# Attention gated by a spatial-shift MLP: small activations in front of more table loads, and a new order of the same instructions

## The chip, the cores and the metric

One of the eight cores of a Trainium2 chip. The metric is the device time of one execution in microseconds (us), median of several runs. Inputs and output are f32.

## What is computed

The reference, cut to what matters (S = 2048 rows, D = 512, H = 32 heads of 16, F = 1376):

```python
xn  = layernorm(x)
# A: linear attention without a mask
q, k, v = split(xn @ wqkv)                     # 32 heads of 16
phi = lambda t: where(t > 0, t + 1, exp(t)) + 1e-6
kv  = phi(k).T @ v;  z = sum(phi(k))           # per head
s   = (phi(q) @ kv / (phi(q) @ z + 1e-6)) @ wo
# B: spatial-shift MLP
h   = gelu(layernorm(xn) @ w1)                 # four quarters of columns, shifted by +1, -1, +2, -2 rows
x1  = xn + shifted(h) @ w2
g   = silu(x1 + gelu(layernorm(x1) @ w3) @ w4)
out = x + s * g
```

## The kernel before

The 2048 rows are 16 tiles of 128, in four quarters of four tiles. Every matmul of full accuracy is made of products of a rounded high part and a low part of each operand (`products`, L343), and many of the 2x2 block products are done with seven products in place of eight (`seven`), whose sums and differences VectorE (DVE) and ScalarE (ACT) make.

The first half of the time goes to layer norms, k, q, the Gram matrices of phi(k) with the rows, and the token mixing (w1, w2). From about 220 us on each quarter b runs through its groups of columns of the 1376: `up_pair` (L1256, w3, GELU), `turn_q` and `forms_q` (phi(q) over its denominator, transposed by way of a round trip to DRAM), `attend_pair` (L1426, the attention rows `so`), `downs` (w4), and last `gate` (L1444), which takes SiLU of the sum (`th<-e`), multiplies by `so` and adds x.

Names that the steps below speak of: `th5_0` and `th10_0` are the SiLU results of row tiles 5 and 10 (L1452, an activation recorded with table 2); `e` is the sum that they read; `p`, `u`, `gf` are copies of PSUM banks (`pb`, `pe`, `pa`) that the seven products of `up_pair` sum in; `so` is the same for the attention; `qr` and `pq` are phi(q)'s two parts from `qv`, a fetch; `yb122h`, `yb122l` are the high and low part of a sum of the layer-normed rows; `w_0h`, `w_0l`, `w_1h`, `w_1l` are sums of blocks of w4, which go to DRAM (`w4t`) and come back; `f_2a`, `f_2sh`, `f_2sl`, `f_3a` are GELU results and their sums; `q9t` is the transposed phi(q) of tile 9, in four fetches from `q9d`, and `q8f`, `q8s0h` are sums of it for the matmuls `pes`, `pbs`; `kt` at the start is k with its mean taken off, which frees the PSUM bank of k for q; `mv` are means. The page leaves the numbers in the names out.

Nothing is emitted as it is written down. `Plan.add` (L99) records 5566 instructions with what each reads and writes. `Plan.emit` (L234) then emits them in the order of a long table, `ORDER`, and gives each tile the slot that a second table, `HOMES`, names: 98 row buffers of 128x512 (tag p), some smaller ones, and eight PSUM banks. Five engines take their own instructions from that order: PE (TensorE), DVE, ACT, POOL, and SP, whose queue issues the DMAs (L217 loads, L221 stores, L225 fetches of what was stored; L229 adds by DMA on POOL). The waits between engines follow from the reads, the writes and the earlier users of a slot.

Activations belong to three tables: Exp, GELU and SiLU (0, 1, 2, L167). Where the table changes, the compiler puts a table load (ACT_TABLE_LOAD) in front of the activation, and the load takes over waits of that activation. `op.warm` (L178) is a one-column activation with the same function, from a constant `tiny` into a column `scr` that nothing reads: it is emitted in front of the real user, so that the load stands in front of it. Before the change `emit` does this (L251) only where the user waits for at least two engines other than ScalarE. `engs` there is the set of engines of the instructions that the user depends on, and of those that used its slot before.

Of the kernel before, what the change touches and what calls it, by code (L numbers as in the profile page):

```python
# [88 lines left out]
class Plan:  # L89
# [144 lines left out]
    def emit(self, order, homes):  # L234
# [3 lines left out]
        table = 0  # L238
        for n in order:
            op = self.ops[n]  # L240
            engs = {o.eng for o in op.pre}
            for t in op.tiles:
                if t.ap is None:
                    tag = t.tag
                    if tag in self.counts:
                        tag += str(next(homes))
                        engs |= users.get(tag, set())
                        users[tag] = t.engs
                    t.ap = self.pools[t.tag].tile([t.rows, t.width], t.dtype, tag=tag, name=t.name)
            if op.table is not None:  # L250
                if op.table != table and len(engs - {"ACT"}) > 1:  # L251
                    op.warm()
                table = op.table
            op.emit()
            for t in op.tiles:
                t.engs.add(op.eng)
# [3 lines left out]
def linear_attn_gated_by_mixer(  # L260
# [1364 lines left out]
    for b in range(NQ):  # L1625
# [499 lines left out]
```

## Time and profile before

| | |
|---|---|
| median of 3 runs | 504.7 us (503.86, 504.7, 506.14) |
| the profiled execution | 504.21 us, its span 502.1 us, TensorE clock 1.0 |
| matmuls, and PE busy | 3204 records, 492.3 us |
| weight loads busy | 446.3 us |
| VectorE, ScalarE, GpSimd busy | 455.2, 400.6, 79.0 us |
| DMA | 124.04 MB, mean 247 GB/s |
| table loads on ScalarE | 27, of which 12 in front of a one-column activation |

How to read it: matmuls overlap, so a busy PE is not a PE at its peak. A matmul of 512 columns follows the one before in 0.23 us and one of 256 columns in 0.12 us where nothing holds it up, though the record of one is 0.28 to 0.40 us long; time is lost where starts lie further apart. In rows of the timeline the columns are start (us), duration (us), engine, line, operation, output and inputs with shapes; in brackets the engine's idle time before it and what released it. A line of the waits says which instruction of which engine waited for which, in total, how often, and the longest.

### The profile page before, as it was taken

The page shows a single profiled execution, that of the slowest core. Times are in us where ns is not written, and L with a number is a line of the kernel's source. Part 1 is how long each engine was busy: PE and PEld are TensorE (multiplying, and loading weights), DVE is VectorE, ACT ScalarE, POOL GpSimd, SP SyncE. Part 2 cuts the span into 40 slices and gives each one's busy share as a digit, 9 for nine tenths or more (in the row PEclk, how much of TensorE's full clock was granted, in tenths as well). Part 3 has the DMA queues.
Part 4 walks back from the last instruction along what each step waited for, and adds up shares of the span by engine and source line. Part 5 has one row for each costly group of instructions (what it writes and reads, how often), then busy time and mean ns, then how long its engine had stood idle before and what let it go on. Part 6 is the DMA issues. An engine that isn't in the chain of part 4 may idle for free.

```text
span 502.1 us, 9824 instructions
## 1 busy us (share of the span) xinstructions
PE 492.3 (98%) x3204; PEld 446.3 (89%) x3204; DVE 455.2 (91%) x977; ACT 400.6 (80%) x874; POOL 79.0 (16%) x98
## 2 busy tenths in 40 slices
PE   8999999999999999999999999999999899999996
PEld 7778878888998889999989999999899899899996
DVE  6999989997899999999999998987899988899966
ACT  6999999967898889879777678757599757799553
POOL 1242222121122201430000002200020011200021
PEclk9999999999999999999999999999999999999999
DMA  7969997698999999899898589998689979879655
GB/s 252 343 162 232 245 241 167 171 262 270 302 315 233 279 295 286 197 277 270 289 319 258 176 240 287 323 233 268 229 194 269 297 210 288 273 195 323 187 97 125
DMA packets 95278, 124.04 MB, mean 247 GB/s; under 512 B 9728, under 2 KB 48156, under 8 KB 95228
## 3 DMA queue, kind: packets, MB, share of 16 engines
q1 hardware_dynamic: 85292, 105.33, 66.2%
q0 software_dynamic: 9936, 18.09, 21.5%
q8 instruction: 25, 0.41, 0.3%
q14 instruction: 25, 0.20, 0.1%
HBM read 78.42 MB, written 35.54 MB: 227 GB/s over the span
## 4 chain that ended last, share of the span: by engine, by line
PE 88%; DMA 5%; ACT 3%; DVE 2%; issue 1%; SPq 0%; ACTq 0%; DVEq 0%
PE a L151 12%; PE pb L151 9%; PE g L151 9%; PE pbk L151 7%; PE acc L151 6%; PE pe L151 5%; PE pbm L151 5%; PE h L151 4%; PE pbs L151 4%; PE uc L151 4%; PE pek L151 3%; PE pa L151 2%; PE pes L151 2%; PE pem L151 2%; PE pbg L151 2%; PE q L151 2%
## 5 line engine op out<-in xcount | busy, mean ns | idle before, releaser
L229 POOL DMA_DIRECT2D th<-in_x x14 | 12.3, 977 | 130.4 <-DVE xo L198 55.7
L229 POOL DMA_DIRECT2D e<-x1d x12 | 10.5, 990 | 100.9 <-DMA q11d<-q11z 39.2
L173 ACT ACT_TABLE_LOAD x15 | 19.2, 1283 | 7.3 <-DVE e L198 3.8
L229 POOL DMA_DIRECT2D zacc<-kr x16 | 17.1, 1069 | 49.8 <-DVE kr L208 17.9
L229 POOL DMA_DIRECT2D o<-x x16 | 14.3, 922 | 56.3 <-ACT o L173 22.5
L173 ACT ACTIVATE gf<-gf 128x256 f32<-128x256 f32 (+1 forms) x50 | 22.3, 457 | 0.5
L491 POOL TENSOR_TENSOR rs<-w,nhalf 128x4 f32<-128x4 f32 (+2 forms) x10 | 12.0, 1205 | 29.9 <-DVE w L203 29.9
L178 ACT ACT_TABLE_LOAD x12 | 15.4, 1283 | 0.2
L198 DVE TENSOR_TENSOR th<-th,so 128x512 f32<-128x512 f32 (+1 forms) x17 | 11.0, 658 | 2.9 <-ACT th L173 2.7
L173 ACT ACTIVATE y<-o,nm,rs 128x512 f32<-128x512 f32 x16 | 12.7, 806 | 0.6 <-DVE nm L208 0.6
L173 ACT ACTIVATE x<-x,nm,rs 128x512 f32<-128x512 f32 x16 | 12.8, 804 | 0.0
L208 DVE SCALAR_TENSOR_TENSOR kr<-kt,kr 128x512 f32<-128x512 f32 x16 | 10.9, 687 | 1.5 <-ACT kr L173 1.1
L173 ACT ACTIVATE p<-pe 128x256 f32<-128x256 f32 x20 | 7.6, 380 | 5.5 <-PE pe L151 5.4
L173 ACT ACTIVATE p<-pb 128x256 f32<-128x256 f32 x20 | 7.6, 380 | 4.9 <-PE pb L151 4.9
L208 DVE SCALAR_TENSOR_TENSOR qz<-pq,zb 128x512 f32<-128x512 f32 x16 | 10.9, 682 | 0.1
L198 DVE TENSOR_TENSOR gf<-pa,p 128x256 f32<-128x256 f32 x20 | 8.3, 417 | 3.0 <-PE pa L151 1.3
L1378 DVE TENSOR_REDUCE den<-qz 128x32 f32<-128x512 f32 x16 | 10.8, 676 | 0.1
L208 DVE SCALAR_TENSOR_TENSOR pq<-pq,rd 128x512 f32<-128x512 f32 x16 | 10.8, 681 | 0.1
L478 DVE BATCH_NORM_STATS2 st<-o 128x6 f32<-128x512 f32 x16 | 10.8, 681 | 0.0
L198 DVE TENSOR_TENSOR e<-a,e 128x512 f32<-128x512 f32 (+1 forms) x17 | 9.9, 590 | 1.0 <-PE a L151 1.0
L198 DVE TENSOR_TENSOR gf<-pb,p 128x256 f32<-128x256 f32 x20 | 8.4, 420 | 2.2 <-PE pb L151 1.7
L173 ACT ACTIVATE pq<-qv,rk 128x512 f32<-128x512 f32 x12 | 8.5, 712 | 2.2 <-DMA w4t<-w_1l 1.4
(1967 smaller groups left out, 2368.8 us busy)
## 6 DMA issues: line engine op xcount, KB each, us to landing
w_s<-in_w SPq DMA_DIRECT2D x36, 256.0 KB
w_t<-w4t SPq DMA_DIRECT2D x32, 256.0 KB
w_b<-w4d SPq DMA_DIRECT2D x30, 256.0 KB
x<-in_x SPq DMA_DIRECT2D x16, 256.0 KB
zacc<-kr POOLq DMA_DIRECT2D x16, 256.0 KB, 6.7
o<-x POOLq DMA_DIRECT2D x16, 256.0 KB, 5.1
w1t<-w1d SPq DMA_DIRECT2D x16, 256.0 KB
x1d<-o SPq DMA_DIRECT2D x16, 256.0 KB
```

What stands on the lines that cost most here:

```text
L151: lambda: nc.tensor.matmul(out.get(), lhs.get(), rhs.get(), start=start, stop=stop, skip_group_check=more))
L173: nc.scalar.activation(out.get(), src.get(), func, scale=get(scale), **kw)
L178: op.warm = lambda: nc.scalar.activation(self.scr[1].get(), self.scr[0].get(), func)
L198: self.vec(eng, out, [a, b], lambda: self.e(eng).tensor_tensor(out.get(), a.get(), b.get(), op=op), True)
L208: lambda: self.nc.vector.scalar_tensor_tensor(out.get(), a.get(), get(s), b.get(), op0=op0, op1=op1),
L229: lambda: self.nc.gpsimd.dma_start(out.get(), get(src), accum_op=ALU.add))
L478: pl.add("DVE", .62, .69, [xv], [st], lambda: nc.vector.bn_stats(st.get(), xv.get()))
L491: lambda: g.tensor_tensor(out.get(), src.get(), nh.get(), op=ALU.pow))
L1378: pl.add("DVE", .6, .68, [t], [den], lambda: nc.vector.tensor_reduce(den.get(), t.get().rearrange("p (h d) -> p h d", d=DH), axis=AX.X, op ...
```

## The change

The condition in `emit` no longer leaves ScalarE out of the set: a small activation now also goes in front of a table change whose user waits for one other engine and for ScalarE itself. `ORDER` and `HOMES` are new tables for the same 5566 instructions: 1738 of the 5566 places hold the same number, and the mean distance that one moved is 2.7 places (the furthest 180); 344 of 1668 entries of `HOMES` are equal. The core of the diff:

```diff
             if op.table is not None:
-                if op.table != table and len(engs - {"ACT"}) > 1:
+                if op.table != table and len(engs) > 1:
                     op.warm()
                 table = op.table
             op.emit()
...
     ORDER = (
         36, 4, 20, 1, 0, 27, 2, 12, 8, 21, 3, 9, 13, 5, 10, 7, 14, 22, 15, 30, 16, 24, 17, 18, 19, 37, 23, 39,
         40, 33, 41, 90, 28, 168, 93, 38, 91, 29, 94, 42, 303, 92, 171, 95, 43, 102, 44, 48, 105, 120, 103, 31,
-        169, 45, 32, 104, 106, 121, 25, 56, 88, 170, 89, 60, 46, 122, 34, 123, 26, 47, 124, 35, 96, 172, 173,
...
```

The number of instructions on PE, VectorE, GpSimd and SP stays. ScalarE keeps its 27 table loads; 19 of them (12 before) stand in front of a small activation. The seven new ones are in front of the users kt8 and kt9 (phi(k) of tiles 8 and 9), f1_0a11, f2_2a11 and f3_0a11 (the first GELU of groups of quarters 1, 2 and 3; f1_0a11 is exchanged with gf1_0, whose load it was), th5_0 and th10_0.

ScalarE at th5_0, near 360 us, before:

```order
L173 ACTIVATE yt42h_5259<-yt4f2_5227 128x512
L173 ACT_TABLE_LOAD
L173 ACTIVATE th5_0_5301<-e11_4573 128x512
L173 ACTIVATE qr8_5314<-qv8_5069,rk_101 128x4x4x32
L173 ACTIVATE p12_0_5316<-pb2_0_5263 128x256
L173 ACTIVATE th6_0_5318<-e12_4720 128x512
```

and now:

```order
L173 ACTIVATE yt42h_5263<-yt4f2_5232 128x512
L178 ACT_TABLE_LOAD
L178 ACTIVATE scr_90<-tiny_86 128x1
L173 ACTIVATE th5_0_5303<-e11_4558 128x512
L173 ACTIVATE qr8_5317<-qv8_5074,rk_101 128x4x4x32
L173 ACTIVATE p12_0_5319<-pb2_0_5260 128x256
L173 ACTIVATE th6_0_5321<-e12_4721 128x512
```

The load moved from th5_0 to the small activation (scr from tiny) ahead of it; what follows keeps its order. At th10_0, near 430 us, it is the same: the load now stands in front of scr, ahead of th10_0, and p13, so11, th9 and u23 keep their places.

PE near 390 us, where the sum a2_10_1 is begun with yb122h (the bank is new to it), before:

```order
L151 MATMUL a3_2_5397<-w4_2_0h_5511,f2_2sh_5737 128x256
L151 MATMUL a3_2_5397<-w4_2_0l_5560,f2_2sh_5737 128x256
L151 MATMUL a2_10_1_5781<-yb122h_5772,w3_lh_3075 96x256
L151 MATMUL pb2_3_5664<-yt32h_5244,w3_3_s1h_3660 128x256
L151 MATMUL pb2_3_5664<-yt32l_5271,w3_3_s1h_3660 128x256
L151 MATMUL pb2_3_5664<-yt32h_5244,w3_3_s1l_3705 128x256
L151 MATMUL a1_2_5437<-w4_2_2_b22_5644,f2_2sh_5737 128x256
L151 MATMUL a2_2_5411<-w4_2_0h_5511,f2_2sl_5739 128x256
```

and now:

```order
L151 MATMUL a3_2_5400<-w4_2_0l_5565,f2_2sh_5742 128x256
L151 MATMUL a3_2_5400<-w4_2_0h_5515,f2_2sl_5744 128x256
L151 MATMUL pb2_3_5667<-yt32h_5246,w3_3_s1h_3662 128x256
L151 MATMUL pb2_3_5667<-yt32l_5280,w3_3_s1h_3662 128x256
L151 MATMUL pb2_3_5667<-yt32h_5246,w3_3_s1l_3720 128x256
L151 MATMUL a1_2_5442<-w4_2_2_b22_5648,f2_2sh_5742 128x256
L151 MATMUL a2_2_5414<-w4_2_0h_5515,f2_2sl_5744 128x256
L151 MATMUL a2_10_1_5809<-yb122h_5778,w3_lh_3076 96x256
L151 MATMUL a2_10_1_5809<-yb122l_5780,w3_lh_3076 96x256
L151 MATMUL a2_10_1_5809<-yb122h_5778,w3_ll_3082 96x256
```

The first matmul of a2_10_1 moved behind six others: w4_2_0h with f2_2sl (two of them, for a3_2 and a2_2), the three of yt32 with w3_3_s1, and w4_2_2_b22 with f2_2sh. On ScalarE at the same place qr10 now goes ahead of pq10, and f2_3a11 ahead of f2_3a22.

VectorE near 16 to 19 us, where kt0 and kt2 take k out of its banks, before:

```order
L198 TENSOR_TENSOR wqt_259<-wq_s0_150,wq_s1_181 128x512
L203 TENSOR_SCALAR w0_280<-mv1_93 128x1
L208 SCALAR_TENSOR_TENSOR kt0_282<-wneg_268,mv1_93,k0_193 128x512
L198 TENSOR_TENSOR wq_1l_293<-wq_s1_181,wq_1h_291 128x512
L203 TENSOR_SCALAR mv1_93<-sx2_289 128x1
L198 TENSOR_TENSOR wqt_259<-wqt_259,wq_s2_195 128x512
L208 SCALAR_TENSOR_TENSOR kt2_317<-wneg_268,mv1_93,k2_146 128x512
```

and now:

```order
L198 TENSOR_TENSOR wqt_245<-wq_s0_150,wq_s1_181 128x512
L203 TENSOR_SCALAR mv1_93<-sx0_257 128x1
L208 SCALAR_TENSOR_TENSOR kt0_284<-wneg_266,mv1_93,k0_194 128x512
L203 TENSOR_SCALAR mv1_93<-sx2_281 128x1
L198 TENSOR_TENSOR wqt_245<-wqt_245,wq_s2_196 128x512
L203 TENSOR_SCALAR w0_296<-mv1_93 128x1
L208 SCALAR_TENSOR_TENSOR kt2_304<-wneg_266,mv1_93,k2_146 128x512
L198 TENSOR_TENSOR wq_1l_306<-wq_s1_181,wq_1h_290 128x512
```

w0 and the low part wq_1l moved behind kt0, wq_1l also behind kt2, and the mean mv1 of tile 0 stands directly ahead of kt0.

Elsewhere: on ScalarE u21_0, near 299 us, stands one place earlier, ahead of th3. On SP, near 401 us, one more fetch (w4_2_10l) stands between the store q9d and the four fetches q9t; the fetch w4_1_0_b21, near 275 us, moved behind the store w4d of w4_8l.

748 rows, old and new, of tables (HOMES, ORDER) are left out of this document.

## The prediction

> **What bounds the kernel now.** I read the page first: the busy shares and the chain of work that ended last.
>
> ```profile
> PE 492.3 (98%) x3204; PEld 446.3 (89%) x3204; DVE 455.2 (91%) x977; ACT 400.6 (80%) x874; POOL 79.0 (16%) x98
> PE 88%; DMA 5%; ACT 3%; DVE 2%; issue 1%; SPq 0%; ACTq 0%; DVEq 0%
> ```
>
> TensorE (PE) sets the time. The change adds and removes no matmul, so all it can give is time in which PE stands still. The waits of PE, grouped by who ended them (total, times, longest), say how much of that the trace names:
>
> ```profile
> PE warm L151 <- POOL ones L379: 1.7, 1, 1.7
> PE a L151 <- ACT pq L173: 1.1, 1, 1.1
> PE pb L151 <- ACT so L173: 0.8, 1, 0.8
> PE pb L151 <- ACT p L173: 0.7, 1, 0.7
> PE q L151 <- DVE mv L203: 0.7, 1, 0.7
> PE uc L151 <- ACT f_3a L173: 0.2, 1, 0.2
> ```
>
> The first is the start, before anything has arrived. The other five are 3.5 us, single events, and I looked for each in the timelines. Last come the table loads of ScalarE (ACT), by the line that caused them (the third column: busy, mean ns; then idle time just before, and its releasers):
>
> ```profile
> L173 ACT ACT_TABLE_LOAD x15 | 19.2, 1283 | 7.3 <-DVE e L198 3.8 <-DVE p1k L198 1.3 <-DVE yt33l L198 1.2
> L178 ACT ACT_TABLE_LOAD x12 | 15.4, 1283 | 0.2
> ```
>
> A load in front of a one-column activation (L178) hardly ever waits; in front of its real user (L173) three of fifteen wait for VectorE (DVE), 3.8, 1.3 and 1.2 us. These three are in reach of the new condition.
>
> **Part 1: the load at 360.74 (th5_0).** ScalarE, VectorE and PE there (start, duration):
>
> ```profile
> 356.35 0.63 ACT L173 ACTIVATE yt42h<-yt4f 128x512 fp32r<-128x512 f32 x1
> 360.74 1.28 ACT L173 ACT_TABLE_LOAD   x1 [3.76 <-DVE e L198]
> 362.03 0.63 ACT L173 ACTIVATE th<-e 128x512 f32<-128x512 f32 x1
> 363.18 0.36 ACT L173 ACTIVATE p<-pb 128x256 f32<-128x256 f32 x1
> ```
> ```profile
> 362.58 0.28 PE L151 MATMUL pe<-yt12h,w_s0l 128*128 128x256 f32 x1
> 363.60 0.39 PE L151 MATMUL pb<-yt22h,w_s0h 128*128 128x256 f32 x1 [0.74 <-ACT p L173]
> ```
>
> The load inherits th's wait for VectorE and stands 3.76 us idle. With a one-column activation ahead, the load runs from about 357.0, and th starts when e is ready, 360.74 instead of 362.03: 1.29 us sooner, and with it qr and p. PE's wait is 0.74; its start-to-start distance is 1.02 where the next matmul of this size follows in 0.12, so the gap costs **0.90** (a wait loses some 0.15 beyond its own length). 1.29 is more than 0.90, so the whole gap goes; the 0.4 left over is slack. A half-way result would need p to be held by its own PE input, and pb is complete long before.
>
> **Part 2: the load at 429.83 (th10_0).**
>
> ```profile
> 428.24 0.39 ACT L173 ACTIVATE p<-pb 128x256 f32<-128x256 f32 x1 [1.37 <-PE pb L151]
> 429.83 1.28 ACT L173 ACT_TABLE_LOAD   x1 [1.21 <-DVE yt33l L198]
> 431.13 0.63 ACT L173 ACTIVATE th<-e 128x512 f32<-128x512 f32 x1
> 431.66 0.37 ACT L173 ACTIVATE so<-pbs 128x256 f32<-128x256 f32 x1
> ```
> ```profile
> 429.07 0.68 DVE L198 TENSOR_TENSOR yt33l<-yt3f,yt33h 128x512 fp32r<-128x512 f32 x1
> ```
> ```profile
> 432.08 0.39 PE L151 MATMUL pb<-yb113h,w_ah 128*128 128x256 f32 x1 [0.75 <-ACT so L173]
> ```
>
> The load can run at 428.63 and end at 429.91; the small activation takes 0.1 more, so th starts at 430.0 instead of 431.13, 1.1 us sooner, and so comes 1.1 us sooner. PE's gap is 0.75 + 0.15 = **0.90** and goes.
>
> The third waiting load (114.74, idle 1.3 behind p1k) has no PE wait near it in the list: 0.
>
> **What the small activations cost.** Seven more, and each takes its place in ScalarE's queue:
>
> ```profile
> 386.72 0.20 ACT L178 ACTIVATE scr<-tiny 128x1 f32<-128x1 f32 x1
> 386.82 0.71 ACT L173 ACTIVATE pq<-qv,rk 128x512 f32<-128x512 f32 x1
> ```
>
> The next instruction starts 0.10 us behind it, so 0.7 us in all on an engine at 80%. Where ScalarE was not idle ahead of the load (f1_0a11 at 299, f2_2a11, f3_0a11 at 434) the user comes 0.1 later. The loads themselves stay 27, the same 1.28 us each. Bounds: 0 to 0.4 on PE; I take 0 here and put it into the allowance below.
>
> By the Trainium skill, "ScalarE: Activation LUTs", section What ACT_TABLE_LOAD costs, a switch of table sets is the load of about 1283 ns and a drain of about 1380 ns, 2.66 us together. The trace has the 1283 but no drain: from the load's start to th's start are 1.29 us (360.74 to 362.03). By the page part 1 would still gain, part 2 not; this is taken up among the rivals.
>
> **Part 3: the new order.** Four exchanges touch gaps of PE. At 390 PE, ScalarE, VectorE and the chain of waits showed:
>
> ```profile
> 384.96 6.07 DMA w4t<-w_1l
> ```
> ```profile
> 391.13 0.72 ACT L173 ACTIVATE pq<-qv,rk 128x512 f32<-128x512 f32 x1 [1.39 <-DMA w4t<-w_1l]
> ```
> ```profile
> 390.08 0.69 DVE L198 TENSOR_TENSOR yb122l<-y_1t,yb122h 128x512 fp32r<-128x512 f32 x1 [0.55 <-ACT w_0h L173]
> ...
> 391.29 0.41 DVE L198 TENSOR_TENSOR gf<-u,pe 128x256 f32<-128x256 f32 x1
> ```
> ```profile
> 390.49 0.28 PE L151 MATMUL a<-w_0l,f_2sh 128*128 128x256 f32 x1
> 391.85 0.33 PE L151 MATMUL a<-yb122h,w_lh 128*96 128x256 f32 x1 [1.08 <-ACT pq L173]
> ...
> 395.25 0.39 PE L151 MATMUL uc<-w_b,f_3a 128*128 128x256 f32 x1 [0.22 <-ACT f_3a L173]
> ```
>
> The wait is put down to pq, but PE's matmul doesn't read pq: it needs yb122 and the bank that gf<-u,pe sets free at 391.70. VectorE is there late: yb122l, ahead of that gf in its queue, takes a slot that the store of w_1h reads, and stores of this stretch land slowly (the row of w_1l's, 6.07 us from its issue, is the nearest). In the new order six matmuls of other sums (w_0h with f_2sl, yt32 with w_s1, w_b22 with f_2sh) stand ahead of a<-yb122h, at 0.12 each **0.7** us of work put into a gap of 1.08 + 0.15. The rest of the gap stays. On ScalarE f2_3a11 now stands ahead of f2_3a22, so the wait at 395.25 (0.22 + 0.15) shrinks, I say by **0.2**. Bounds for both: 0, if a matmul moved ahead waits itself, to 1.6.
>
> At 299 ScalarE's u stood last ahead of the load, and PE waited for its bank:
>
> ```profile
> 298.98 0.36 ACT L173 ACTIVATE u<-pb 128x256 f32<-128x256 f32 x1
> ```
> ```profile
> 299.02 0.28 PE L151 MATMUL pa<-yb211h,w_al 128*128 128x256 f32 x1
> 299.40 0.39 PE L151 MATMUL pb<-yt31h,w_s1h 128*128 128x256 f32 x1
> ```
>
> 0.38 from start to start is 0.26 over the pace. u now stands one place earlier, ahead of a 0.5 us activation: **0.3** back.
>
> At the start kt on VectorE frees the bank for q:
>
> ```profile
> 18.30 0.74 DVE L208 SCALAR_TENSOR_TENSOR kt<-wneg,mv,k 128x512 f32<-128x512 f32 x1
> ```
> ```profile
> 19.09 0.50 PE L151 MATMUL q<-wq_0h,u_0h 128*128 128x512 f32 x1 [0.74 <-DVE mv L203]
> ```
>
> wq_1l (0.7 us) moves from ahead of this kt to behind it, so kt starts about 0.6 sooner; some of PE's work of that stretch moves too, so I count **0.4** of 0.9, bounds 0 and 0.9.
>
> **The sum.** 0.90 + 0.90 + 0.7 + 0.2 + 0.3 + 0.4 = 3.4 us. Against it: the order puts a consumer nearer to its producer at three other places (PE's peg near 124, uc near 470, pb near 474), and the small activations cost something; I charge three waits of the smallest size in the list, 0.2 each: 0.6. That leaves 2.8. The profiled execution took 504.2 (span 502.1): 501.4 for its like. It lay 0.5 under the median of 504.7, so the median is forecast at **501.9**. About 0.5%, 2.5 us, is what a measurement of this kernel can tell from no change: the forecast lies just beyond. Own range 500.4 to 503.3: all bounds of gain with no new waits at one end, half the gain at the other.
>
> **Rivals.**
> - *The exchanges give nothing.* PE's queue is full of reordered work; each moved matmul may meet its own wait. Then only the two loads count: 1.8 less 0.6, **503.5**. For it: DVE is 91% busy. Against: the moved matmuls read operands that lay ready in the trace. 0.11.
> - *The 362 gain is given back at 390.* If the store's landing (6.07 us from issue) clocks that stage, PE arrives 0.9 sooner and waits 0.9 longer: 2.8 less 0.9, **502.8**. Against: the stores are issued behind ScalarE's and VectorE's work, which moves with PE. 0.12.
> - *The change doesn't do what it says.* The activation may inherit the wait itself, or another wait on the load's path (a fetch for qr behind th) ends at the same moment; exchanges nothing: **504.7**. Against: scr and tiny are touched by nothing else late. 0.06.
> - *A drain with each load.* If a load that starts right behind other work held ScalarE for a second 1.28 us, th at 429 would be released at 428.63 + 2.57 = 431.2, no sooner than the 431.13 of now, and part 2 would give nothing: 2.8 less 0.9, **502.8**. The trace speaks against it: scr starts at 386.72, right behind a load, and pq 0.10 later. 0.03. The page of the Trainium skill named above (ScalarE: Activation LUTs) would have it so.
> - *Slower: a fetch comes late.* SP's queue has one more fetch (w_10l) ahead of q9t's four, and q9t feeds VectorE and then PE:
>
> ```profile
> 400.89 0.90 SPq L225 DMA_DIRECT2D q9t<-q9d  x2
> ```
> ```profile
> 405.96 0.42 DVE L198 TENSOR_TENSOR q8f<-q9t 128x256 f32<-128x256 f32 x1
> ```
> ```profile
> 407.94 0.28 PE L151 MATMUL pes<-m_t1h,q8s0h 128*128 128x256 f32 x1
> ```
>
> Two issues take 0.90, so the last goes out 0.45 later, at about 401.8, and must land by 405.96: 4.2 us, then PE stalls. With the 6.07 us of the store it lands at 407.9, 1.9 late, and what VectorE does behind it too; with the gains lost as well, 504.7 + 1.9 = **506.6**, and more if it meets a second one. It decides from a landing of 4.2 us on. For it: DMA engines are busy nearly throughout. Against: before, with 4.6 us, nobody waited, and these fetches are 64 KB. 0.08. By the Trainium skill, "DMA: Bandwidth & Descriptors", a transfer has about 2.0 us of fixed cost and then its bytes at 436 KB per us, some 2.2 us here as an estimate, with which nothing would stall; the 6.07 us of the store speak against it in this stretch.
>
> **How the numbers follow.** The forecast keeps 0.60. The range 500.4 to 505.0 holds it nearly whole, and the first four rivals but for the upper half of the third; it leaves out the slower one and the tails, about 0.15 to 0.2. Faster by over 0.5% means under 502.2: some 0.65 of the forecast's 0.60, and 0.03 from the cases at 502.8, 0.42. Slower means over 507.2: the upper part of the last rival and what I can't see, 0.06. Within 0.5%: 0.52.
>
> **What would show it.** Right: 19 small activations in front of loads; only one load with an idle time of over half a us before it; the waits pb<-p and pb<-so gone from PE's list; the wait at 390 at 0.5 or less; th5_0 starting within 0.1 of the end of e. Wrong, if PE's list has the old waits under new names (pb held by another activation, VectorE's gf later), if the sum of PE's gaps is unchanged, or if a q fetch stands among PE's or VectorE's releasers.

## The result, and the profile after

| | before | after |
|---|---|---|
| median | 504.75 us (503.86 to 506.14, 6 runs) | 501.62 us (501.14 to 502.23, 6 runs) |
| ratio | | 0.9937, 95% interval 0.9922 to 0.9952 |
| profiled execution, its span | 504.21, 502.1 us | 502.23, 500.2 us |

The change makes the kernel 0.63% faster, 3.1 us, where 2.8 us were forecast. The two profiled executions lie only 2.0 us apart; that difference is taken up at the end of the account below.

The same lines of the page after the change:

```profile
PE 492.2 (98%) x3204; PEld 444.4 (89%) x3204; DVE 455.9 (91%) x977; ACT 401.5 (80%) x881; POOL 79.9 (16%) x98
PE 91%; DMA 4%; DVE 2%; ACT 2%; SPq 1%; issue 1%; DVEq 0%
```

The busy time of PE is what it was, and its share of the chain rises from 88 to 91%, while ScalarE's falls. The waits of PE after:

```profile
PE warm L151 <- POOL ones L379: 1.7, 1, 1.7
PE pb L151 <- DVE gf L198: 0.9, 1, 0.9
PE k L151 <- ACT wk_0h L173: 0.3, 1, 0.3
PE q L151 <- DVE kt L208: 0.2, 1, 0.2
```

The waits for p, so, pq and f_3a are gone. A new one has come, pb for VectorE's gf, 0.9. The table loads:

```profile
L178 ACT ACT_TABLE_LOAD x19 | 24.4, 1283 | 0.3
L173 ACT ACT_TABLE_LOAD x8 | 10.3, 1283 | 0.9 <-PEq L2117 0.8
```

Loads that wait for VectorE are no longer there. ScalarE at th5_0 and PE at the place where it waited 0.74:

```profile
358.20 1.28 ACT L178 ACT_TABLE_LOAD   x1
359.49 0.20 ACT L178 ACTIVATE scr<-tiny 128x1 f32<-128x1 f32 x1
361.20 0.64 ACT L173 ACTIVATE th<-e 128x512 f32<-128x512 f32 x1 [1.50 <-DVE e L198]
...
362.52 0.39 ACT L173 ACTIVATE p<-pb 128x256 f32<-128x256 f32 x1
```
```profile
363.15 0.28 PE L151 MATMUL pe<-yt12h,w_s0l 128*128 128x256 f32 x1
363.26 0.28 PE L151 MATMUL pb<-yt22h,w_s0h 128*128 128x256 f32 x1
```

The load is over 1.7 us before e is ready, and PE goes from one matmul to the next in 0.11. At th10_0 it is the same:

```profile
427.50 0.39 ACT L173 ACTIVATE p<-pb 128x256 f32<-128x256 f32 x1 [1.46 <-PE pb L151]
427.90 1.28 ACT L178 ACT_TABLE_LOAD   x1
429.20 0.20 ACT L178 ACTIVATE scr<-tiny 128x1 f32<-128x1 f32 x1
429.31 0.62 ACT L173 ACTIVATE th<-e 128x512 f32<-128x512 f32 x1
429.83 0.36 ACT L173 ACTIVATE so<-pbs 128x256 f32<-128x256 f32 x1
```
```profile
430.35 0.28 PE L151 MATMUL pb<-yb113h,w_ah 128*128 128x256 f32 x1
430.47 0.40 PE L151 MATMUL a<-w_9l,f_9h 128*128 128x512 f32 x1
```

Here th follows scr in 0.11, 1.82 us sooner than before in absolute time and 1.1 sooner behind p (427.50 to 429.31; before 428.24 to 431.13), and PE's matmul has no wait.

At 390 PE now reads:

```profile
390.78 0.28 PE L151 MATMUL a<-w_0h,f_2sl 128*128 128x256 f32 x1
391.21 0.33 PE L151 MATMUL a<-yb122h,w_lh 128*96 128x256 f32 x1
...
392.67 0.27 PE L151 MATMUL a<-yb222h,w_lh 128*96 128x256 f32 x1
393.84 0.38 PE L151 MATMUL pb<-yt42h,w_b 128*128 128x256 f32 x1 [0.89 <-DVE gf L198]
```

The gap in front of a<-yb122h has fallen from 1.24 over the pace to 0.31, as the exchange was to do, and 1.5 us later stands a gap of 1.05 that the profile of before doesn't have. VectorE's gf, and the chain of waits at that place, name the cause of 0.64 of it:

```profile
393.36 0.42 DVE L198 TENSOR_TENSOR gf<-pb,p 128x256 f32<-128x256 f32 x1 [0.64 <-DMA q8d<-q8z]
```
```profile
387.12 6.15 DMA q8d<-q8z
```

gf takes the slot of q8z, which a store still reads until 393.27. The store was issued at 387.12, some 3 us ahead of the matmuls that were exchanged, so their order does not reach it.

### The profile page after: what moved, and what is told of

Same layout as the page of the kernel before. It is cut to its first block, busy times and chain, and to the rows that moved or that the text cites. A ratio compares the mean times of both kernels' runs of the same rounds, so it can differ in the third digit from the quotient of the medians.

```text
span 500.2 us, 9836 instructions
## 1 busy us (share of the span) xinstructions
PE 492.2 (98%) x3204; PEld 444.4 (89%) x3204; DVE 455.9 (91%) x977; ACT 401.5 (80%) x881; POOL 79.9 (16%) x98
## 4 chain that ended last, share of the span: by engine, by line
PE 91%; DMA 4%; DVE 2%; ACT 2%; SPq 1%; issue 1%; DVEq 0%
PE a L151 14%; PE pb L151 10%; PE g L151 9%; PE pbk L151 7%; PE acc L151 6%; PE pe L151 5%; PE pbm L151 5%; PE h L151 4%; PE pbs L151 4%; PE uc L151 4%; PE pek L151 3%; PE pa L151 2%; PE pbg L151 2%; PE pem L151 2%; PE pes L151 2%; PE pak L151 2%
## 5 line engine op out<-in xcount | busy, mean ns | idle before, releaser
L229 POOL DMA_DIRECT2D zacc<-kr x16 | 18.2, 1139 | 54.2 <-DVE kr L208 23.7
L491 POOL TENSOR_TENSOR rs<-w,nhalf 128x4 f32<-128x4 f32 (+2 forms) x10 | 13.9, 1393 | 27.7 <-DVE w L203 27.7
L173 ACT ACTIVATE u<-pb 128x256 f32<-128x256 f32 x20 | 7.5, 377 | 5.6 <-PE pb L151 5.5
L198 DVE TENSOR_TENSOR gf<-u,pe 128x256 f32<-128x256 f32 x20 | 8.3, 413 | 1.7 <-PE pe L151 1.5
```

The lines of the kernel that those rows point to most:

```text
L173: nc.scalar.activation(out.get(), src.get(), func, scale=get(scale), **kw)
L198: self.vec(eng, out, [a, b], lambda: self.e(eng).tensor_tensor(out.get(), a.get(), b.get(), op=op), True)
L229: lambda: self.nc.gpsimd.dma_start(out.get(), get(src), accum_op=ALU.add))
L491: lambda: g.tensor_tensor(out.get(), src.get(), nh.get(), op=ALU.pow))
```

## The experiments

All times are medians, beside the kernel before on the same chip. Positions on PE are in the table that follows the runs.

**The condition without the order, and the order without the condition.** The first two kernels split the change:

```diff
 cond_only (the kernel before)
-                if op.table != table and len(engs - {"ACT"}) > 1:
+                if op.table != table and len(engs) > 1:
 order_only (the changed kernel)
-                if op.table != table and len(engs) > 1:
+                if op.table != table and len(engs - {"ACT"}) > 1:
```

> The kernel before with the new condition alone: old order, old slots, six more small activations. My theory (two table loads are worth the two PE waits of 0.9 us at 362 and 431; the exchanges of the order are worth the rest): 502.9 us, the gaps at 362.6 and 431.1 gone, those at 18, 299, 390 and 395 still there. Rival A (the new order and slots carry the gain, the activations are hidden anyway): 504.5. Rival B (the activations carry all of it): 501.6.

> The changed kernel with the old condition: new order, new slots, no new small activation. My theory: 503.4 us, with PE waits of about 0.7 at 362 and 431, and the gaps at 18 and 299 small. Rival A (order and slots carry the gain): 501.6. Rival B (activations alone): 504.7.

Measured: cond_only 501.6 us, ratio 0.9936 (0.9923 to 0.9949); order_only 503.19, ratio 0.9968 (0.9955 to 0.9982). My theory gave the order its time (503.4, where rival B had 504.7), and fell at the condition: the condition alone is as fast as the whole change (rival B), 3.0 us and not 1.8. The two parts don't add up: alone they are worth 3.0 and 1.4, together 3.1. In order_only's waits the two of the loads are back, and the new one at 393 is there too:

```profile
PE pb L151 <- DVE gf L198: 1.2, 2, 0.8
PE pb L151 <- ACT so L173: 0.7, 1, 0.7
PE pb L151 <- ACT p L173: 0.6, 1, 0.6
```

**Only two of the small activations.** By number, th5_0 is instruction 3880 and th10_0 4740:

```diff
 two_only; th5_only and th10_only name one number each
-                if op.table != table and len(engs - {"ACT"}) > 1:
+                if op.table != table and (n in (3880, 4740) or len(engs - {"ACT"}) > 1):
```

> The kernel before with a small activation added in front of th5_0 and th10_0 alone. My theory: 502.9 us, the same as with the new condition at every place, since the other small activations cost ScalarE 0.1 us each beside PE. If they cost something on the path, this one is 0.1 to 0.6 us faster than the kernel with all of them; if th5_0 and th10_0 aren't what matters it stays at 504.7.

Measured 501.67 us, ratio 0.9941 (0.9928 to 0.9953): the same as cond_only. So these two activations carry what the condition brings, and the others neither cost nor give anything that can be seen with both of them there. That each of the two does its part:

> The kernel before with a small activation in front of th5_0 alone. In the trace PE reaches the matmul at 363 0.93 us sooner, by the first matmul of kv; if the time follows the trace: 503.6 us (0.9 less). If the two activations are worth the 2.9 us that both together showed in the times, 503.0 (half of it), or all of it if this one alone also ends what makes the runs of before spread over 2.7 us: 501.8.

> The kernel before with a small activation in front of th10_0 alone. By the trace PE is 1.03 us sooner from 408 to its last matmul: 503.5 us. If each of the two is worth half of the 2.9 us: 503.0. No other stage of PE should change.

Measured: th5_only 503.54, ratio 0.9983 (0.9971 to 0.9995), 1.0 us below its 504.53; th10_only 503.06, ratio 0.9976 (0.9966 to 0.9986), 1.5 us. The intervals hold the 0.93 and 1.03 of the trace, and half of 2.9 in each, too. Neither carries it alone. The runs of th5_only spread from 502.05 to 505.53, those of th10_only from 502.65 to 503.53. In the profiled execution of th5_only PE gives its gain back at 390:

```profile
389.49 0.28 PE L151 MATMUL a<-w_0l,f_2sh 128*128 128x256 f32 x1
391.09 0.33 PE L151 MATMUL a<-yb122h,w_lh 128*96 128x256 f32 x1 [1.31 <-DVE gf L198]
```

It arrives earlier than before and waits 1.31 where the four executions of before waited 0.64 to 1.15.

**One exchange on PE alone.** The condition, and the first matmul of a2_10_1 (4391) moved to its second (4392):

```diff
 pe390 (the kernel before, with the new condition)
-        ..., 4365, 4391, 4273, 4274, ...
+        ..., 4365, 4273, 4274, ..., 4366, 4391, 4392, ...
```

> The kernel before with the new condition, and of all exchanges only the one on PE at 390: the first matmul of a2_10_1 behind the next matmuls of other sums, ahead of its second one. If this exchange is worth 0.7 us as predicted: 500.9, with the gap of 0.73 at 389 gone and nothing later. My theory now: the stage ends with the landing of the store q8d<-q8z, which VectorE's gf waits for and PE behind it, so the gap moves: 0.1 to 0.2 at 389, and 0.8 to 1.0 at 392 in place of 0.34; 501.6, the same as with the condition alone.

Measured 502.2 us, ratio 0.995 (0.993 to 0.9971), no better than the condition alone. PE's three gaps at this place, start to start and less the pace of 0.12 (the first stands in front of a<-yb122h, the second in front of pb<-yt42h, the third in front of uc<-w_b,f_3a):

| kernel | 390 | 393 | 395 | together |
|---|---|---|---|---|
| before | 1.24 | 0.00 | 0.38 | 1.62 |
| before_b | 1.32 | 0.00 | 0.00 | 1.32 |
| before_c | 0.90 | 0.11 | 0.86 | 1.87 |
| before_d | 0.80 | 0.49 | 0.09 | 1.38 |
| cond_only | 0.73 | 0.34 | 0.58 | 1.65 |
| pe390 | 0.30 | 0.86 | 0.66 | 1.82 |
| after | 0.31 | 1.05 | 0.00 | 1.36 |
| after_b | 0.00 | 1.47 | 0.04 | 1.51 |

Against cond_only the first gap has shrunk by 0.43, and the two behind it have grown by 0.60:

```profile
393.12 0.38 PE L151 MATMUL pb<-yt42h,w_b 128*128 128x256 f32 x1 [0.70 <-DVE gf L198]
...
394.59 0.39 PE L151 MATMUL uc<-w_b,f_3a 128*128 128x256 f32 x1 [0.50 <-ACT f_3a L173]
```

So the wait moved on, as expected, and the three together are no shorter. The chain there names the same store, but VectorE shows that the store is little of it here:

```profile
386.72 5.83 DMA q8d<-q8z
```
```profile
391.84 0.69 DVE L208 SCALAR_TENSOR_TENSOR pq<-pq,qr 128x512 f32<-128x512 f32 x1 [0.24 <-ACT qr L173]
392.64 0.42 DVE L198 TENSOR_TENSOR gf<-pb,p 128x256 f32<-128x256 f32 x1
```

The store lands at 392.55, as pq ends (392.53). The next instruction behind a pq starts 0.6 after it elsewhere in this stretch, so gf comes about 0.2 later for the store; the rest of the 0.86 is VectorE's own queue, with pq held 0.24 by ScalarE's qr. In after VectorE stood 0.64 idle for the store, in after_b 0.79.

**The store's slot.** The changed kernel, with the slots of two tiles exchanged:

```diff
 slot390 (HOMES)
-        gf2_8: 4 (that of q8z), f2_3a12: 92
+        gf2_8: 92, f2_3a12: 4
```

> The changed kernel with the slots of two tiles exchanged, gf2_8 and f2_3a12: gf2_8 no longer takes the slot that the store q8d<-q8z still reads at 393.3. Theory: that store's landing is what VectorE's gf waits for, and so PE's 0.89 at 393.8; the gf then runs at 392.7, PE's wait there falls to about 0.25, and some 0.4 of the 0.65 comes back as a wait for f2_3a11, whose table load stands behind pq11 and its fetch: 501.4 (gain 0.2), at most 501.0. Rival: gf is held by something else (its own bank, the reciprocal ahead of it): the wait of 0.89 stays, 501.6.

Measured 502.01 us with a spread from 500.72 to 505.57, ratio 0.9959 (0.9941 to 0.9977): no gain, and nothing that separates 501.4 from 501.6. The profiled execution was the one of 505.57. gf no longer waits for the store of q8z in it, as the theory has it, yet PE's gap in front of pb<-yt42h is still 0.86 over the pace (1.05 in after) and not 0.25: another store holds w_0l, which stands ahead of gf in VectorE's queue.

```profile
392.88 0.69 DVE L198 TENSOR_TENSOR w_0l<-w_fa,w_0h 128x512 fp32r<-128x512 f32 x1 [0.61 <-DMA w4t<-w_1l]
...
394.44 0.36 DVE L198 TENSOR_TENSOR gf<-pb,p 128x256 f32<-128x256 f32 x1
```

Behind that the fetch qv is late, which pq11 on ScalarE waits for, and with it the load and f_3a, for which PE waits 0.79:

```profile
386.53 7.30 DMA qv<-pqd
```
```profile
393.92 0.72 ACT L173 ACTIVATE pq<-qv,rk 128x512 f32<-128x512 f32 x1 [0.40 <-DMA qv<-pqd]
```

With the one store out of the way something else of the queue ends last. Right behind these two waits of PE its granted clock is 0.50 from 397.0 to 400.3, and matmuls of 256 columns follow in 0.21 in place of 0.12, which costs some 1.5 us:

```profile
397.40 0.41 PE L151 MATMUL uc<-w_b,f_3a 128*128 128x256 f32 x1
397.61 0.41 PE L151 MATMUL a<-yb222l,w_lh 128*96 128x256 f32 x1
```

In no other profiled execution does the clock fall between 10 and 490 us; what made it fall here no run shows. The three longest of the twelve executions (503.93, 504.86, 505.57) are those with a mean granted clock of 0.995 or 0.996; the other nine lie between 500.72 and 502.83, around 501.55. So the long times go with the clock, and on the price of the slot the run is inconclusive.

**The kernels themselves again.** Three more profiles of before and one more of after:

> The kernel before itself, profiled a second time. In the first profiles the kernel before took 0.36 us less than the median of its runs, and each other kernel 0.5 to 0.9 us more than its own, so the two profiles differ by 2.0 us where the medians differ by 3.0. If the first profile of before was a short one by chance, this one is near 505.2 us and shows about 1 us more of PE's idle time than the first, at places outside 362 and 431. If profiles are good to 0.3 us, it is 504.2 again and the missing 1 us must lie in what a profile doesn't show.

> The kernel before itself, profiled a third time: as for the second, 505.2 us on average of both if the first was short by chance, 504.2 if not. The gaps of PE at 362, 390 and 431 in it tell which of them are there in every execution.

> The changed kernel itself, profiled a second time: 502.0 us, with PE's gaps at 18 (0.35), 24 (0.3) and 392 (1.0) as in its first profile if they belong to the kernel, and the 0.4 us of the first 5 us gone if they were chance.

> The kernel before against itself: 504.5 us and a ratio of 1.000, with a spread of 2 us as in the runs of before so far. If it came out 0.5 us or more below the runs it is compared with, part of the 3 us would belong to the way of comparing and not to the change.

Measured: before_b 503.62, before_c 504.06, after_b 503.01; before_d 504.69 as a median, ratio 1.0004 (0.9996 to 1.0013), its profiled execution 504.69. The idea that the first profile of before was short by chance fell: four profiled executions average 504.15, 0.4 under the median of about 504.5. The comparison itself is sound to 0.1%. PE's gap at 362 (0.90 or 0.91) and the one at 431 (0.90 to 0.93) are in all four; the one at 390 goes from 0.80 to 1.32. After_b has the new gap at 393 again, 1.47, and 0.5 in all over the pace between 20 and 30 us, as after and order_only have; before has under 0.1 there in all four.

**No small activation at all.**

```diff
 no_warm (the kernel before)
-                if op.table != table and len(engs - {"ACT"}) > 1:
+                if op.table != table and n < 0:
```

> The kernel before with no small activation at all: all 27 loads stand in front of their users, 11 with a wait in place of 5. If an exposed load costs PE what the trace shows (0.9 us at two of five places): six more, of which two or three reach PE, 506.5 to 507.5, and the profiled execution lies as far above the profiled one of before as the median above the median. If an exposed load costs more in executions without a profile, the median rises by about 1.5 times what the profile rises by.

Measured 505.69 us, ratio 1.0021 (1.0012 to 1.0031), 1.2 us slower, and a profiled execution of 504.49, 0.3 above the mean of before's. I had expected two to three us. ScalarE has now 27 such loads, and they idle 10.0 us in place of 7.3:

```profile
L173 ACT ACT_TABLE_LOAD x27 | 34.6, 1283 | 10.0 <-DVE e L198 3.8 <-DVE p1k L198 1.3 <-DVE yt33l L198 1.2
```

The three longest are the same as before. Two of the new ones wait for VectorE too, 0.94 at 66.39 and 0.83 at 393.84, and PE waits behind both: 0.4 for p5k near 69 us, where before had no wait, and 0.8 for f_3a, where the executions of before have 0 to 0.7. The small activations that were there already were worth 1.2 us; the two that matter here, 2.9.

**Where PE was, and when.** Starts on PE in each profiled execution: the first matmul of kv, the one at 363 (pb<-yt22h,w_s0h), the one at 408 (pes<-m_t1h,q8s0h), and the last; then the three stretches between them.

| kernel | kv | 363 | 408 | last | kv to 363 | 363 to 408 | 408 to last |
|---|---|---|---|---|---|---|---|
| before | 209.97 | 363.60 | 407.94 | 497.33 | 153.63 | 44.34 | 89.39 |
| before_b | 209.70 | 363.27 | 407.47 | 496.77 | 153.57 | 44.20 | 89.30 |
| before_c | 209.72 | 363.34 | 407.82 | 497.17 | 153.62 | 44.48 | 89.35 |
| before_d | 210.02 | 363.60 | 408.52 | 497.82 | 153.58 | 44.92 | 89.30 |
| th5_only | 209.83 | 362.78 | 407.98 | 497.50 | 152.95 | 45.20 | 89.52 |
| th10_only | 210.91 | 364.49 | 408.01 | 496.24 | 153.58 | 43.52 | 88.23 |
| two_only | 210.06 | 362.74 | 407.00 | 495.28 | 152.68 | 44.26 | 88.28 |
| cond_only | 209.50 | 362.20 | 406.96 | 495.31 | 152.70 | 44.76 | 88.35 |
| order_only | 209.62 | 363.58 | 408.18 | 497.39 | 153.96 | 44.60 | 89.21 |
| after | 210.66 | 363.26 | 407.21 | 495.51 | 152.60 | 43.95 | 88.30 |
| after_b | 211.16 | 363.93 | 408.03 | 496.32 | 152.77 | 44.10 | 88.29 |
| pe390 | 209.84 | 362.49 | 407.14 | 495.48 | 152.65 | 44.65 | 88.34 |
| slot390 | 210.92 | 364.52 | 410.59 | 498.91 | 153.60 | 46.07 | 88.32 |
| no_warm | 210.24 | 364.09 | 408.30 | 497.66 | 153.85 | 44.20 | 89.36 |

The first stretch is 0.6 to 1.0 shorter where th5_0 has its activation, the last 1.0 to 1.1 where th10_0 has it, and only there. Slot390 has both and is the exception in the first: its gap at 363 is gone too, but between 210 and 363 it loses 1.0 elsewhere, some 0.2 each at 270, 299 and 303 among it. The middle stretch, which holds the stage of the stores, is anything from 43.5 to 45.2, whatever was done (slot390 has 46.07, with the 1.5 of the lower clock in it). The time to kv goes from 209.5 to 211.2, and not by the change alone: th10_only, the same as before up to there, has 210.91.

## Why the prediction was right, point by point

- **Part 1, right.** 0.90 forecast; from kv to 363 the trace gives 153.6 before and 152.6 to 153.0 with the activation (153.6 without it in th10_only), but for slot390. In the times it is 1.0 with an interval of 0.25 to 1.5.
- **Part 2, right.** 0.90 forecast, 1.0 to 1.1 in the trace, 0.7 to 1.7 in the times.
- **The small activations, right.** They were put at nothing, and two_only and cond_only differ by 0.1.
- **Part 3, wrong.** 1.6 us were expected of the exchanges. With the activations there they are worth nothing that can be measured (501.62 against 501.6, good to about half a us); without them the new order and slots gave 1.4 in the times, which no stretch of order_only's trace shows. The step that failed is the one that counts a gap as gained when its own cause is taken away, without asking for the next thing late there, which the text did ask at 362. At 390 the first gap did shrink by 0.93, and the next came to 1.05, 0.64 of it VectorE's wait for the store of q8z; with the 0.38 at 395, that went, 0.3 of 0.9 was gained. Over all executions nothing is left of it: the three gaps add up to 1.3 to 1.9 in the four of before and to 1.4 and 1.5 in the two of after. PE's new wait, pb for VectorE's gf, is one of the signs of being wrong that the prediction names. At 299 the gap of PE is gone, and another stands 3 us later, 0.35 from start to start in front of a matmul that followed in 0.13 before:

```profile
301.65 0.28 PE L151 MATMUL pe<-yt11h,w_s0l 128*128 128x256 f32 x1
302.00 0.39 PE L151 MATMUL pb<-yt41h,w_b 128*128 128x256 f32 x1
```

  At the start the wait for kt is 0.18 in place of 0.74 (0.4 to 1.1 in the other executions of before), and the time is lost again in what follows; the first g starts 0.49 behind a matmul that the next follows in 0.23 elsewhere, and PE reaches kv at 210.66 and 211.16, no sooner than before's 209.70 to 210.02:

```profile
18.93 0.50 PE L151 MATMUL q<-wq_0h,u_0h 128*128 128x512 f32 x1 [0.18 <-DVE kt L208]
...
23.94 0.40 PE L151 MATMUL q<-wq_1h,u_1l 128*128 128x512 f32 x1
...
24.43 0.97 PE L151 MATMUL g<-k0h,x0h 128*128 128x512 f32 x3
```
- **The rival that was nearest.** "The 362 gain is given back at 390" is what the profile of th5_only shows (its middle stretch is 45.20, before's average 44.49: 0.7 of 0.9), and the new wait behind a store is its mechanism. It does not hold in the times of the whole change, nor in its traces: the middle stretch averages 44.35 in the five profiles that have both activations (after, after_b, cond_only, two_only, pe390). The drain behind a load (the Trainium skill, "ScalarE: Activation LUTs", section What ACT_TABLE_LOAD costs) is not there after the change either: the load ends at 429.18, scr starts at 429.20 and th at 429.31. A late q9t is in none of the lists; after the change the trace gives 3.9 us from its issue to its landing, under the 4.2 from which that rival counts.
- **The sum.** 2.8 forecast, 3.1 measured, and two errors offset each other: the two activations give 2.9 in the times where 1.8 was put, and the exchanges nothing where 1.0 was left after the allowance. That the total came so near is luck; the two loads and their places are not.
- **What stays open.** The trace accounts for 1.9 of the 2.9: on average over the five profiles with both activations (slot390 left out) the first stretch is 0.9 shorter than before's and the last 1.0. The executions as a whole average 502.4 against before's 504.15, 1.7 apart, since the five come to kv 0.4 later and win 0.1 in the middle. The medians are 3.0 apart: the kernels with both lie 0.1 to 1.4 above their own median in the profile, and before lies 0.4 under it. no_warm goes the same way, 0.3 in the profile and 1.2 in the times. That a load which is exposed costs more in an execution without a profile fits these, but not order_only, which hides no load, is 1.4 us faster in the times and no faster in the profile (504.06). The other candidate, that the stage of the stores varies more in executions without a profile (before spreads over 2.7 us, cond_only over 1.1), was not tried by itself; slot390 was to touch it and stayed unclear. The granted clock does not explain it: the executions of before with a mean clock of 0.998 average 504.5, those with 1.0 average 504.8. I can't tell the two candidates apart.

## What to carry to other kernels

A table load takes over the wait of the activation behind it, so an idle time in front of a load is worth looking at, and a one-column activation ahead of it costs 0.1 us of ScalarE; but only those loads count that stand last before a wait of the engine that sets the end, here two of fifteen. Two gaps that are caused by different instructions of the same stage don't add up: before a gap is counted as gained, read from the trace when the next releaser there ends, above all a DMA that was issued before the instructions that are to move, as the store of q8z was here. When an effect is of a per cent or less, compare many plain executions: here the profiles were the better tool for the place, and not for the size.

## What the runs showed that I had not expected

The store of q8z took 5.8 to 6.3 us from issue to landing in the six executions whose chain names it, that of w_1l 6.1 to 7.2 in three, and the fetch qv 5.5 and 7.3 in two, so a stage that ends with them can vary by a us from one execution to the next; on PE it took 43.5 to 45.2 us. A granted clock of 0.50 for 3.4 us, in one profiled execution of fourteen, cost 1.5 us, half of what the whole change gives. And a profiled execution can lie on either side of the median of its kernel: 0.4 under it for before, 1.2 under it for no_warm, 0.1 to 1.4 above it for the kernels with both activations (slot390 left out).
